# The last group of a dynamic convolution and MLP kernel: its tokens loaded in a turned order by eight DMAs, the last chunk stored by one DMA each

## The chip, the core and the metric

The kernel runs on one core of a Trainium2 chip. TensorE (PE) multiplies matrices, VectorE (DVE) and ScalarE (ACT) do elementwise work, GpSimd (POOL) does little here, and SyncE (SP) issues nearly all DMAs, one after the other, in program order. Sixteen DMA engines move the data. The metric is the device time of one execution in microseconds (us).

## The reference

```python
# x (8, 4096, 192), weight_gen (8, 4096, 8, 7), moe_w_in (192, 2048), moe_w_out (2048, 192), float32
w = softmax(weight_gen, axis=-1)                      # 7 taps for each token and head
out[b, s, h, :] = sum_k w[b, s, h, k] * x_pad[b, s + k, h, :]   # causal, 8 heads of 24 channels
t = out.reshape(32768, 192)
h = t @ w_in
return (relu(h) ** 2) @ w_out                         # (32768, 192) float32
```

Every token gets a weighted sum of itself and its six predecessors, channel by channel, and then goes through a two-layer network with a squared ReLU.

## The kernel before

Token number p*256 + r lies on partition p (of 128) in row r (of R = 256), so each partition holds 256 neighbouring tokens. The work goes in 64 chunks (NCH) of four rows (TC), that is 512 tokens (N). Two chunks share a load group (TG = 8 rows): `load_group(gi)` brings the group's tap logits `wt` (line 116) and its x rows with six rows of halo `xt` (line 117). Two groups' buffers exist. Below, "chunk c" is counted from 0 to 63; chunks 62 and 63 form the last group, gi = 31.

For a chunk, VectorE and ScalarE form the softmax and the tap sums (the convolution). VectorE then transposes blocks (line 402, into `xr`), and SP writes `xr` to a DRAM scratch `xd` (four DMAs, line 408) and reads it back channel-major as `xT` (two DMAs, line 413, which wait until the four have landed). ScalarE splits `xT` into a rounded part `xh` (line 316) and VectorE the remainder `xl` (line 319). These are the moving operands of the first matrix product.

The main loop has eight steps (j) of a chunk. In each, TensorE does `mm1` (line 439, 18 matmuls that read `xh` and `xl` of this chunk) and `mm2_turned` (line 512, 20 matmuls) of the step two back; ScalarE does `relu` (456), `square` (460) and `high` (464), VectorE `low` (468). Every engine runs its instructions in the order written. The convolution of chunk c + 2 is spread from step 3 of chunk c to step 3 of chunk c + 1, its transposes and the DRAM round trip follow, and the split lines 316 and 319 stand in step 6 of the chunk before the one that needs them, ahead of that step's `high`. `load_group((c + 3) // 2)` is issued at step 0 of each odd chunk c; the last group is loaded in chunk 59.

`mm1` and `mm2_turned` read their moving operand through `two_streams`, which takes each run of 32 token columns as two streams of 16 in turn. Each such read therefore moves token 16*i + m of a run of 32 to place 2*m + i. Chunks 1 to 62 are read twice that way; `store_turned` brings their result back through 24 small DMAs (line 540) into `o_sb`, and `put_out` with `reads = 2` undoes the order on the way to DRAM by four DMAs, one for each 32 partitions. The last chunk uses `mm2` with the tokens on the output's partitions, so it has one such read: `store(c, t0, t1)` calls `put_out` with `reads = 1`, again four DMAs. In the last chunk the rows go out in three steps: rows 0 and 1, then row 2, then row 3, each as soon as `finish` has summed it (line 561; for the very last row line 780).

In `put_out` the view `"(q a b r) d -> q b a r d"` makes b the outermost loop of each of the four DMAs: 8 turns for `reads = 2`, 16 for `reads = 1`. Line 77 is its `dma_start`.

Of the kernel before, what the change touches and what calls it, by code (L numbers as in the profile page):

```python
# [21 lines left out]
def kernel(  # L22
# [9 lines left out]
    nc = tc.nc  # L32
# [4 lines left out]
    P = 128  # L37
    Q = 32
    HALO = K - 1
    R = B * S // P  # L40
    PPB = S // R
    TC = 4
    NCH = n_chunks or R // TC
    TG = 8
    CPG = TG // TC
# [26 lines left out]

    def put_out(c, t0, t1, o_sb, reads):
        rows = slice(rows_of(c) + t0, rows_of(c) + t1)
        v = out.rearrange("(q a b r) d -> q b a r d", q=P // Q, a=2 ** reads, r=R)
        for q in range(P // Q):
            nc.sync.dma_start(out=v[q, :, :, rows, :], in_=o_sb[q * Q:(q + 1) * Q, t0:t1])
# [15 lines left out]
    def rows_of(c):  # L93
        return (c + CPG if c < CPG else c - CPG if c < 2 * CPG else c) * TC
# [8 lines left out]
    def load_group(gi):  # L103
        t0 = rows_of(gi * CPG)
        xt = xin.tile([P, TG + HALO, D], F32, name="xt")
        wt = xin.tile([P, TG, H, K], F32, name="wt")
        x_tiles[gi], w_tiles[gi] = xt, wt
        wf = wt.rearrange("p t h k -> p t (h k)")
        if gi == 0:
            nc.sync.dma_start(out=wf[:, 0:TC, :], in_=wg_v[:, t0:t0 + TC, :])  # L110
            nc.sync.dma_start(out=xt[:, HALO:HALO + TC, :], in_=x_v[:, t0:t0 + TC, :])
            for h in (HALO // 2, 0):
                nc.sync.dma_start(out=xt[:, h:h + HALO // 2, :], in_=x_v[:, t0 - HALO + h:t0 - HALO // 2 + h, :])
            return
        if t0 > 0:
            nc.sync.dma_start(out=wf, in_=wg_v[:, t0:t0 + TG, :])
            nc.sync.dma_start(out=xt, in_=x_v[:, t0 - HALO:t0 + TG, :])
            return
        nc.gpsimd.memset(xt[:, 0:HALO, :], 0.0)
        nc.sync.dma_start(out=wf, in_=wg_v[:, 0:TG, :])  # L120
        nc.sync.dma_start(out=xt[:, HALO:, :], in_=x_v[:, 0:TG, :])
        for p0 in range(0, P, PPB):
            nc.sync.dma_start(
                out=xt[p0 + 1:p0 + PPB, 0:HALO, :],
                in_=x_v[p0:p0 + PPB - 1, R - HALO:R, :],
            )
# [398 lines left out]
    def store_turned(c, part):  # L525
        X = works[c]
        if part == 0:
            o_sb = op.tile([P, TC, D], F32, name="o_sb", bufs=2)
            Y = stage.tile([P, 2, N], F32, name="raw")
            outs[c] = o_sb, Y  # L530
            nc.vector.transpose(Y[:, 0], X[:, 0])  # L531
        else:
            nc.vector.tensor_tensor(out=X[0:D1, 1], in0=X[0:D1, 1], in1=X[0:D1, 2], op=ALU.add)
            nc.vector.transpose(outs[c][1][0:D1, 1], X[0:D1, 1])  # L534
        o_sb, Y = outs[c]
        y = Y[:, part].rearrange("p (t q i) -> p q t i" if c < N_PE else "p (q t i) -> p q t i", t=TC, i=Q)
        for e in range(P // Q if part == 0 else D1 // Q):
            d0 = part * P + e * Q
            for q in range(P // Q):
                nc.sync.dma_start(  # L540
                    out=o_sb[q * Q:(q + 1) * Q, :, d0:d0 + Q],
                    in_=y[e * Q:(e + 1) * Q, q],
                )
        if part:
            put_out(c, 0, TC, o_sb, 2)

    outs = {}

# [12 lines left out]
                nc.vector.tensor_tensor(out=to[:, h], in0=acc[:, h], in1=tmp[:, t, l], op=ALU.add)  # L561

    def store(c, t0, t1):
        put_out(c, t0, t1, outs[c][0], 1)


    nc.vector.memset(warm, 0.0)
    nc.scalar.activation(warm, warm, AF.Exp)
    load_group(0)
    eps_terms(0)  # L570
    make_identity(nc, ident)
# [29 lines left out]
    for u in range(NU):  # L601
# [45 lines left out]
        for i in range(3 if u == 0 else 4):  # L647
            relu(0, 4 * u + i)
    load_group(1)
    lace(NU + 1, 1, 2, 3)  # L650
    for f in conv1[3:6]:
# [63 lines left out]
    for c in range(1, NCH):  # L715
        tail = c == NCH - 1
        for j in range(NJ):
            if j == 0 and c % 2 and (c + 3) // 2 * CPG < NCH:
                load_group((c + 3) // 2)
            if j == CONV_BEG and 1 < c < NCH - 2:  # L720
                plan_conv(c + 2, *conv_steps(c + 2, 0))
            if c == 1 and j == 0:
                for t in range(TC // 2):
                    finish(0, t)
                store(0, 0, TC)
# [23 lines left out]
            if c > 1 and j == OUT_STEP:  # L749
                store_turned(c - 1, 0)  # L750
            if c > 1 and j == OUT_STEP + 1:
                store_turned(c - 1, 1)
# [4 lines left out]
    c = NCH - 1  # L757
# [7 lines left out]
    for t in range(TC - 1):  # L765
        for fb in range(NF - 4, NF):
            mm2_tile(c, fb, t)
        finish(c, t)
        if t:
            store(c, 0 if t == 1 else t, t + 1)  # L770
# [7 lines left out]
    o_sb, tmp = outs[c]  # L778
    finish(c, t, tmp[:, t, 0:D])
    nc.vector.tensor_tensor(out=o_sb[:, t], in0=rest[:, 0:D], in1=tmp[:, t, 0:D], op=ALU.add)  # L780
    store(c, t, TC)


# [28 lines left out]
```

## Time and profile before

| | us |
|---|---|
| time of three runs, median | 2145.14 (2144.61 to 2146.45) |
| the profiled execution | 2143.92 |
| its span, first to last instruction | 2142.2 |
| PE busy | 2131.4 (99%) |
| DVE busy | 1857.5 (87%) |
| ACT busy | 1797.9 (84%) |
| mean granted TensorE clock | 0.999 of full speed |

The profiled execution takes 1.7 us more than its span and lies 1.2 us below the median of the runs. A row of a timeline gives the start, the duration, engine, line, operation, what it writes from what, and in brackets the engine's idle time before it and what ended that. SPq is SP's sequencer, where a row is the issue of a DMA, not its transfer. A row of windows gives a stretch, its length, the busy time of each engine with its instruction count, the granted clock, the DMA engines' busy share and the rate in GB/s.

### The profile page before, as it was taken

How to read it: one execution, taken by the hardware profiler on the slowest of the kernel's cores; microseconds unless marked ns; L12 is line 12 of the kernel's file. 1: busy time of each engine (PE TensorE's matmuls, PEld its weight loads, DVE VectorE, ACT ScalarE, POOL GpSimd, SP SyncE). 2: the span in 40 equal slices, each digit the busy share in tenths (PEclk: the TensorE clock that was granted, in tenths of full speed). 3: DMA queues.
4: the chain of work that ended last, by engine and by line, in shares of the span. 5: the costliest groups of instructions: out<-in, count | busy, mean ns of one | idle time of the engine just before them, and what ended most of it. 6: DMA issues, size and time to landing. Idle time of an engine off the chain costs nothing.

```text
span 2142.2 us, 50282 instructions
## 1 busy us (share of the span) xinstructions
PE 2131.4 (99%) x19486; PEld 2044.4 (95%) x19486; DVE 1857.5 (87%) x2866; ACT 1797.9 (84%) x3492; POOL 9.9 (0%) x18
## 2 busy tenths in 40 slices
PE   9999999999999999999999999999999999999998
PEld 9889999999999999999999999999999999999998
DVE  9988988888889888888898888888988888889884
ACT  8888888888888888888888888888888888888886
POOL 0000000000000000000000000000000000000000
PEclk9999999999999999999999999999999999999999
DMA  8433334333233332333433333334333233333231
GB/s 230 100 80 102 88 66 104 88 96 92 62 105 93 91 105 62 93 102 84 103 89 66 104 87 97 91 63 104 91 93 104 62 92 94 91 104 87 67 76 39
DMA packets 324303, 195.33 MB, mean 91 GB/s; under 512 B 225128, under 2 KB 282472, under 8 KB 320224
## 3 DMA queue, kind: packets, MB, share of 16 engines
q1 hardware_dynamic: 322768, 188.58, 34.9%
q0 software_dynamic: 1296, 3.54, 0.9%
q8 instruction: 152, 2.49, 0.5%
q14 instruction: 87, 0.71, 0.1%
HBM read 106.39 MB, written 49.55 MB: 73 GB/s over the span
## 4 chain that ended last, share of the span: by engine, by line
PE 96%; DVE 1%; SPq 1%; ACT 1%; DMA 0%; issue 0%; DVEq 0%; ACTq 0%
PE acc L512 49%; PE ph L439 45%; PE acc L476 1%; PE acc L485 1%; SPq L540 1%; DMA xT<-xd 0%; DVE gl L468 0%; ACT gh L464 0%; ACT rg L460 0%; DMA out_dram<-o_sb 0%; ACT rg L456 0%; DVE du L184 0%; DVE du L186 0%; PE acc L439 0%; DVE xl L319 0%
## 5 line engine op out<-in xcount | busy, mean ns | idle before, releaser
L512 PE MATMUL acc<-gh,V 64*128 64x512 f32 x5952 | 1085.2, 377 | 0.0
L512 PE MATMUL acc<-gl,V 64*128 64x512 f32 x3968 | 917.4, 378 | 0.6 <-DVE gl L468 0.5
L439 PE MATMUL ph<-xh,W 64*128 64x512 f32 x6084 | 917.7, 376 | 0.2
L512 PEld LDWEIGHTS acc<-gh,V 64*128 64x128 f32 x5952 | 779.9, 186 | 25.6
L468 DVE TENSOR_TENSOR gl<-rg,gh 128x512 fp32r<-128x512 f32 x1008 | 641.3, 675 | 119.6 <-ACT gh L464 119.6
L439 PEld LDWEIGHTS ph<-xh,W 64*128 64x128 f32 x6084 | 709.8, 186 | 24.8 <-issue 0.7
L456 ACT ACTIVATE rg<-ph 128x512 f32<-128x512 f32 x992 | 537.8, 594 | 218.1 <-PE ph L439 217.4
L460 ACT ACTIVATE rg<-rg 128x512 f32<-128x512 f32 x1008 | 579.8, 631 | 0.2
L512 PEld LDWEIGHTS acc<-gl,V 64*128 64x128 f32 x3968 | 556.3, 186 | 23.6 <-DVE gl L468 3.3
L464 ACT CAST gh<-rg 128x512 fp32r<-128x512 f32 x1008 | 574.2, 624 | 3.2 <-PE acc L485 3.2
L439 PE MATMUL ph<-xl,W 64*128 64x512 f32 x3042 | 459.3, 376 | 0.0
L275 DVE TENSOR_TENSOR pr<-xt,wt 128x768 f32<-128x768 f32 (+1 forms) x441 | 411.1, 945 | 2.3
L439 PEld LDWEIGHTS ph<-xl,W 64*128 64x128 f32 x3042 | 355.3, 186 | 11.6
L288 DVE TENSOR_TENSOR pr<-pr 128x768 f32<-128x768 f32 x366 | 345.8, 945 | 0.1
L319 DVE TENSOR_TENSOR xl<-xT,xh 128x512 fp32r<-128x512 f32 x186 | 117.5, 687 | 123.0 <-ACT xh L316 120.2
L316 ACT CAST xh<-xT 128x512 fp32r<-128x512 f32 x186 | 102.6, 622 | 1.8 <-DMA xT<-xd 1.7
L246 ACT ACTIVATE wt<-wt 128x224 f32<-128x224 f32 x62 | 24.2, 391 | 94.8 <-DVE wt L245 94.8
L522 DVE TENSOR_TENSOR raw<-acc,raw 128x512 f32<-128x512 f32 x124 | 79.0, 675 | 3.8 <-ACT raw L520 3.8
L520 ACT COPY raw<-acc 128x512 f32<-128x512 f32 x124 | 66.5, 596 | 0.0
L402 DVE STREAM_TRANSPOSE xr<-pr 128x768 f32<-128x768 f32 x62 | 60.7, 978 | 2.1
L534 DVE STREAM_TRANSPOSE raw<-raw 64x512 f32<-64x512 f32 x62 | 43.6, 704 | 2.1
L531 DVE STREAM_TRANSPOSE raw<-raw 128x512 f32<-128x512 f32 x62 | 43.7, 704 | 0.0
(93 smaller groups left out, 450.4 us busy)
## 6 DMA issues: line engine op xcount, KB each, us to landing
xT<-xd SPq DMA_DIRECT2D x124, 384.0 KB
xt<-in_x_dram SPq DMA_DIRECT2D x30, 1344.0 KB
out_dram<-o_sb SPq DMA_DIRECT2D x252, 96.0 KB
xd<-xr SPq DMA_DIRECT2D x248, 96.0 KB
o_sb<-raw SPq DMA_DIRECT2D x1488, 16.0 KB
raw<-raw SPq DMA_DIRECT2D x62, 128.0 KB
wt<-in_weight_gen_dram SPq DMA_DIRECT2D x31, 224.0 KB
raw<-in_moe_w_in_dram SPq DMA_DIRECT2D x16, 192.0 KB
```

The costliest lines, as they stand in the source:

```text
L275: tt(out=dst, in0=src, in1=wf[:, t0 * H:t1 * H, k:k + 1].broadcast_to([P, m, G]), op=ALU.mult)
L288: tt(out=prs[k0], in0=prs[k0], in1=prs.pop(k), op=ALU.add)
L316: nc.scalar.copy(parts["h"][:, k, n], src[k][:, n])
L319: tt(out=parts["l"][:, k, n], in0=src[k][:, n], in1=parts["h"][:, k, n].bitcast(F32), op=ALU.subtract)
L439: nc.tensor.matmul(two[i], w, two_streams(xx[rows, k]), start=(n == 0), stop=(n == len(seq) - 1))
L456: nc.scalar.activation(r, ph, AF.Relu)
L460: nc.scalar.activation(r, r, AF.Square)
L464: nc.scalar.copy(gh, rgs[c, fb])
L468: nc.vector.tensor_tensor(out=gl, in0=rgs.pop((c, fb)), in1=ghs[c, fb].bitcast(F32), op=ALU.subtract)
L512: nc.tensor.matmul(accs[c][b + h], w, two_streams(g[rows]), **fl)
L520: nc.scalar.copy(X[:, k], acc[b])
L522: nc.vector.tensor_tensor(out=X[:, k], in0=acc[b + 1], in1=X[:, k], op=ALU.add)
```

## The change

For the last group alone, `load_group` reads DRAM through `"(q b a r) d -> q a b r d"` with a = 2: within each run of 32 partitions, partition 16*a + b gets the tokens of row block 2*b + a. Logits and x are loaded by four DMAs each, one for every 32 partitions, eight in place of two. After one read through `two_streams` the tokens of chunk 63 then stand in plain order, so `store` calls `put_out` with `reads = 0` for it, a single DMA over 128 partitions. Chunk 62 is read twice, so it now needs `reads = 1`. Chunk 0 keeps `reads = 1`.

```diff
     def put_out(c, t0, t1, o_sb, reads):
         rows = slice(rows_of(c) + t0, rows_of(c) + t1)
+        if reads == 0:
+            nc.sync.dma_start(out=out.rearrange("(p r) d -> p r d", r=R)[:, rows, :], in_=o_sb[:, t0:t1])
+            return
         v = out.rearrange("(q a b r) d -> q b a r d", q=P // Q, a=2 ** reads, r=R)
         for q in range(P // Q):
             nc.sync.dma_start(out=v[q, :, :, rows, :], in_=o_sb[q * Q:(q + 1) * Q, t0:t1])
@@ load_group
+        if gi == NCH // CPG - 1:
+            turned = "(q b a r) d -> q a b r d"
+            x_t = x.rearrange("b s d -> (b s) d").rearrange(turned, q=P // Q, a=2, r=R)
+            wg_t = wg.rearrange("b s h k -> (b s) (h k)").rearrange(turned, q=P // Q, a=2, r=R)
+            for src, dst, r0 in ((wg_t, wf, t0), (x_t, xt, t0 - HALO)):
+                for q in range(P // Q):
+                    nc.sync.dma_start(out=dst[q * Q:(q + 1) * Q], in_=src[q, :, :, r0:t0 + TG, :])
+            return
@@ store_turned
-            put_out(c, 0, TC, o_sb, 2)
+            put_out(c, 0, TC, o_sb, 1 if c >= NCH - CPG else 2)
@@ store
-        put_out(c, t0, t1, outs[c][0], 1)
+        put_out(c, t0, t1, outs[c][0], 1 if c == 0 else 0)
```

## Rows read from the trace of the kernel before

**Rows 1.** The page: the chain that ended last, by engine.

```profile
PE 96%; DVE 1%; SPq 1%; ACT 1%; DMA 0%; issue 0%; DVEq 0%; ACTq 0%
```

**Rows 2.** Timeline of SP's DMA issues, last chunk to the end, and the last issue.

```profile
2112.41 16.15 SPq L540 DMA_DIRECT2D o_sb<-raw  x24
2128.66 10.99 SPq L77 DMA_DIRECT2D out_dram<-o_sb  x16
...
2139.06 0.59 SPq L77 DMA_DIRECT2D out_dram<-o_sb  x1
```

**Rows 3.** Timeline of VectorE at the end: the sums of rows 2 and 3.

```profile
2132.72 0.42 DVE L561 TENSOR_TENSOR o_sb<-acc,raw 128x128 f32<-128x128 f32 x2 [0.72 <-ACT raw L558]
...
2133.69 0.36 DVE L780 TENSOR_TENSOR o_sb<-ph,raw 128x192 f32<-128x192 f32 x1
```

**Rows 4.** Windows after TensorE's last matmul: granted clock and DMA share.

```profile
2137.00:2138.00 1.00, 0.00 (x0) 0.00 (x0) 0.00 (x0) 0.00 (x0) 0.00 (x0) 0.74 0.20 49
2138.00:2139.00 1.00, 0.00 (x0) 0.00 (x0) 0.00 (x0) 0.00 (x0) 0.00 (x0) 0.50 0.10 25
```

**Rows 5.** Timeline of SP's issues in chunk 59, around the last group's load.

```profile
1975.19 0.44 SPq L116 DMA_DIRECT2D wt<-in_weight_gen_dram  x1
1975.67 0.42 SPq L117 DMA_DIRECT2D xt<-in_x_dram  x1
...
1979.14 1.94 SPq L408 DMA_DIRECT2D xd<-xr  x4
1984.61 1.32 SPq L413 DMA_DIRECT2D xT<-xd  x2
```

**Rows 6.** The same view for chunk 60, which has no load.

```profile
2012.09 1.80 SPq L408 DMA_DIRECT2D xd<-xr  x4
2015.61 1.31 SPq L413 DMA_DIRECT2D xT<-xd  x2
```

**Rows 7.** The page's DMA issues: sizes of the transfers.

```profile
xt<-in_x_dram SPq DMA_DIRECT2D x30, 1344.0 KB
...
xd<-xr SPq DMA_DIRECT2D x248, 96.0 KB
...
wt<-in_weight_gen_dram SPq DMA_DIRECT2D x31, 224.0 KB
```

**Rows 8.** Windows in chunk 59 while the load runs: DMA share and GB/s.

```profile
1978.00:1979.00 1.00, 1.00 (x13) 1.00 (x11) 0.97 (x2) 1.00 (x3) 0.00 (x0) 1.00 0.90 366
1979.00:1980.00 1.00, 1.00 (x13) 1.00 (x11) 1.00 (x3) 0.44 (x1) 0.00 (x0) 1.00 1.06 419
...
1983.00:1984.00 1.00, 1.00 (x13) 1.00 (x11) 0.93 (x4) 1.00 (x3) 0.00 (x0) 1.00 0.07 19
```

**Rows 9.** Windows in the output stores: chunk 61's (two rows), chunk 0's (one row).

```profile
2102.50:2102.60 0.10, 0.10 (x4) 0.10 (x2) 0.10 (x1) 0.10 (x2) 0.00 (x0) 1.00 0.60 246
2103.30:2103.40 0.10, 0.10 (x5) 0.10 (x3) 0.10 (x1) 0.10 (x2) 0.00 (x0) 1.00 0.60 246
58.70:58.80 0.10, 0.10 (x4) 0.10 (x2) 0.10 (x1) 0.10 (x1) 0.10 (x1) 1.00 1.44 307
```

**Rows 10.** Timeline of SP and ACT where the split waited for `xT`.

```profile
1391.82 1.32 SPq L413 DMA_DIRECT2D xT<-xd  x2
...
1397.83 1.66 ACT L316 CAST xh<-xT 128x512 fp32r<-128x512 f32 x3 [0.24 <-DMA xT<-xd]
```

**Rows 11.** Timelines of ACT, PE and DVE, end of chunk 59 and start of 60.

```profile
1991.63 1.65 ACT L316 CAST xh<-xT 128x512 fp32r<-128x512 f32 x3
...
1995.68 0.94 PE L439 MATMUL ph<-xh,W 64*128 64x512 f32 x6
...
1997.87 0.48 PE L512 MATMUL acc<-gl,V 64*128 64x512 f32 x2
...
1992.28 1.90 DVE L319 TENSOR_TENSOR xl<-xT,xh 128x512 fp32r<-128x512 f32 x3 [2.01 <-ACT xh L316]
1997.17 1.24 DVE L468 TENSOR_TENSOR gl<-rg,gh 128x512 fp32r<-128x512 f32 x2
```

## What the change was predicted to do, and why

> **What bounds the kernel now.** I read the chain that ended last first: it lies on TensorE for 96% of the span [rows 1], so time can be won or lost in two ways only, by letting TensorE stand idle or by what comes after its last matmul. The second is seen in the timeline of SP's issues at the end, beside that of VectorE. The last sum of the kernel, line 780, ends at 2133.69 + 0.36 = 2134.05 [rows 3], but SP issues its last store only at 2139.06, as the last of 16 issues of line 77 that follow each other without a gap from 2128.66 on, 10.99 / 16 = 0.69 us each [rows 2]. The span ends at 2142.2, so 3.14 us after the last issue. The tail is thus bound by SP's issue rate, for about five us, and the change cuts that count.
>
> The first way needs the chunk in which the load is issued. I looked there for what follows the load in SP's queue: the DRAM round trip of the next chunk's operand, lines 408 and 413 [rows 5], then for the first instruction that needs it (line 316 on ScalarE) and for the first matmul behind that (line 439) [rows 11]. That path has almost no slack, as the next part shows.
>
> **The stores: removed issues.** Chunk 62 keeps four stores, now 16 turns of the outer loop instead of 8. Chunk 63 goes from twelve issues to three. SP comes to chunk 62's stores at 2128.66 and leaves them at about 2128.66 + 4 * 0.69 = 2131.4 [rows 2]. Rows 0 and 1 are summed at 2132.00 (VectorE stood idle for 0.72 before 2132.72) and are issued then; row 2 is summed at 2133.14, row 3 at 2134.05 [rows 3]. Each single issue is over before the next sum, so the last one starts at about 2134.1 in place of 2139.06: 4.96 earlier. It carries four times the data, 98 kB in place of 25: at the 392 GB/s that the load's two steady windows average [rows 8] that is 0.25 against 0.06 us, so 0.2 is given back. **Gain at the end: 4.7 us** (4.2 if a 128-partition issue or its landing takes 0.5 longer than the rows here; 5.0 at most, since the sum of row 3 doesn't move).
>
> **The loads: added issues.** Six more issues at the pitch of 0.48 us (1975.19 to 1975.67) are 2.9 us more of SP [rows 5]. Line 523 was issued behind the load and moves by that much. Line 408 was held by its own input until 1979.14; now SP reaches it at about 1975.67 + 0.47 + 2.9 + 0.6 = 1979.6, half a us later. From line 413's issue to the split, where the split did wait for it, it took 1397.83 - 1391.82 = 6.0 us [rows 10]. So in chunk 59 `xT` was there at 1984.61 + 6.0 = 1990.6 and the split came at 1991.63 [rows 5, 11]: 1.0 us of slack covers the half us. The issues alone cost nothing; without that cover they would cost 0.5.
>
> **The loads: how wide they run.** This is the term that decides. The trace of before holds no load whose outermost loop has two turns, so I bound it from both sides. The store views say how the outermost loop bears on width: while chunk 61's stores run (outer loop 8), the DMA share stands at 0.60 and 246 GB/s in window after window; while chunk 0's run (outer loop 16, the same 3072 bytes for a partition), it goes to 1.44 and 307 GB/s [rows 9]. So the outer loop of 8 kept about half of the engines busy. The turned load walks `a` (2 turns) outermost on its DRAM side. The nearest rows therefore speak for two engines of 16, for each of the eight DMAs, and I take that; the other end is all 16, as for lines 116 and 117, with no cost.
>
> On two engines: the load is 1344 + 224 KB = 1606 kB [rows 7]. The steady windows moved 366 and 419 GB/s, 392 in the mean, 24.5 for one of 16 engines [rows 8]. Two engines move 49 GB/s, so the load lasts 32.7 us (30.6 by the faster window, 35.1 by the slower) in place of some 4. With data flowing about 1.0 us after the first issue, an estimate, it ends at 1975.19 + 1.0 + 32.7 = 2008.9.
>
> The Trainium skill, "DMA: Bandwidth & Descriptors", section "Why a DMA increments its semaphore by 16 and not by 1", says that a DMA issued from SP runs on the largest number of engines up to 16 that divides the outermost counts of both its sides, on the lowest-numbered ones: here two, the same two for all eight DMAs. By that rule the sum is the one above; the trace agrees as far as its stores go (half of the busy share at eight turns), and no run here shows which engines they are.
>
> **What that holds up.** `xr` to `xd` (line 408) goes on the same queue, spread over all engines, so part of each of its four DMAs stands behind the load on those two. In before the load already held it: line 413 came 5.47 us after line 408 with the load ahead and 3.52 without [rows 5, 6]. Now, after 2008.9, the two engines still have their sixteenth each of lines 523 and 408 to move, 1.3 us at 24.5 GB/s (four DMAs of 96 KB [rows 7] and, by the code, 64 partitions of 512 floats), and line 413 followed the last traffic of 1983 to 1984 by under a us [rows 5, 8]; I take 0.8. Line 413 is issued at 2011.0 in place of 1984.61, and `xT` is there 6.0 later, at 2017.0. The split at 1991.63 becomes 2017.0: **25.4 us late**.
>
> On ScalarE everything of chunk 59's last two steps is queued behind that split, on VectorE line 319 and all behind it. TensorE can go on to 1995.68, where chunk 60's first `mm1` wants `xh` [rows 11]. It then stands idle until 2017.6. Of the 25.4, nothing is absorbed: in before the first `gl` that `mm2` needs after that `mm1` was ready at 1997.17 + 0.7 = 1997.87, and its matmul started at 1997.87 [rows 11]. VectorE's chain from the split to it is unchanged, so that matmul moves by the full 25.4.
>
> The clock: after TensorE's last matmul the granted clock went from 1.00 (2.4 GHz) to 0.50 (1.2 GHz) within the window 2137 to 2138, less than 4.5 us after the engine stopped [rows 3, 4]. A pause of 21.9 us will do the same. At half rate chunk 60's first `mm1` takes 3.9 us instead of 1.94 and still ends before the `gl` that comes next, at 2023.3; so that much is covered. How much longer the clock stays low no row shows: between nothing and one step at half rate, 4.1 us (a chunk of eight steps is 2012.09 - 1979.14 = 32.95 [rows 5, 6]). I take nothing.
>
> A second stall isn't due: after line 413 SP has chunk 58's 24 small DMAs, four stores and line 523 to catch up on, 16.15 + 2.8 + 0.6 us [rows 2], and is free at 2032, before the next line 408 at 2012.09 + 25.4. x of the last group is wanted from step 3 of chunk 60 on, later than it lands.
>
> **Sum.** +25.4 - 4.7 = +20.7 us. Against the profiled execution (2143.92, span 2142.2 and 1.7 around it) 2164.6; that execution lies 1.2 below the median of the runs, so 2165.8, and I predict 2166.
>
> **Rivals.** First, *the load is spread over all engines* after all, because what counts is the SBUF side with its 32 partitions. Then the added issues are hidden as shown, and only the tail remains: 2145.14 - 4.7 = 2140.4, 0.22% faster. For it: transfers of 32 partitions stand all over the trace (lines 408, 540). Against it: chunk 61's stores have 32 partitions on the SBUF side too, and ran at half width [rows 9]. It decides where the load ends by 1991.63 - 6.0 - 2.1 = 1983.5 with the steps of the sum, so from nine engines up. The Trainium skill, same page, "Rules for kernel authors", says of two transfers to disjoint halves of the partitions that both still spread over all 16 engines; by that rule it would be this case, and the stores' rows speak against it.
>
> Second, *the two engines change from DMA to DMA*, or the queue lets line 408 past the load. With four pairs at work the load lasts 1606 kB / 196 GB/s = 8.2 us, line 413 comes at 1975.19 + 1.0 + 8.2 + 2.1 = 1986.5, the split at 1992.5 in place of 1991.63: 0.9 late. That gives 2145.14 - 4.7 + 0.9 = 2141.3, within 0.2%. For it only that no row tells the engines apart; against it that line 408 did wait behind the load in before [rows 5, 6].
>
> **How the numbers follow.** About 0.2% (4.3 us) is what a measurement of this kernel can tell from no change. The forecast gets 0.85, the first rival 0.08, half of it beyond 0.2% faster and half within; the second 0.06, 0.05 of that within 0.2% and 0.01 faster; another stall that I don't see 0.01. So faster 0.05, same 0.09, slower 0.86. The range is that of the forecast: low with the faster window's rate, data 0.4 us sooner and the full 5.0 of the tail, 2145.14 + 25.4 - 2.5 - 5.0 = 2163, less a few us for a shorter way from `xd` to the split, 2159; high with the slower rate, the clock's 4.1 and a tail of 4.2, 2145.14 + 25.4 + 2.4 + 4.1 - 4.2 = 2173, with 1 for the spread of the runs 2174.
>
> **What would show it.** In the changed profile: the DMA share in chunk 59 stands near 2/16 for some 30 us; line 413's issue comes near 2011; line 316 is preceded by a long idle time ended by the DMA `xT<-xd`; TensorE has one gap of over 20 us at chunk 60's first `mm1`, with the granted clock at 0.50 in it; and at the end the last line 77 is issued within 0.2 us of line 780's end. If the share reaches 1 during the load, the first rival holds and the time is near 2140. If the gap is there but the tail still shows issues without a gap, the stores' term is wrong.

## The result and the profile after

The changed kernel takes 2165.49 us, the median of four runs (2163.88 to 2167.15), against 2144.88 (2144.23 to 2146.45) for the kernel before. The ratio is 1.0095, with a 95% interval from 1.0078 to 1.0113: slower by 20.6 us. Lines have moved: 408, 413 and 316 of before are 419, 424 and 327 of after; 439 is 450, 512 is 523, 468 is 479, 540 is 551; the new load is line 124, a store of four DMAs is line 80 and the single store line 76.

The profiled execution of after took 2167.15, with a span of 2165.4. It was already 3.6 us behind the profiled execution of before where it came to the load (first issue at 1978.80, in before at 1975.19 [rows 5]), in a stretch where the two programs are the same. Times below are therefore compared from the first issue of the load on.

The page of after, the chain that ended last by engine, answers to [rows 1]. TensorE's share has gone from 96 to 89%, and DMA and VectorE have taken it.

```profile
PE 89%; DVE 4%; DMA 3%; ACT 2%; SPq 1%; issue 1%; DVEq 0%; ACTq 0%
```

The timeline of SP's issues in chunks 59 and 60 of after answers to [rows 5, 6]: start, duration, line, what is written from what, and the number of issues.

```profile
1978.80 2.65 SPq L124 DMA_DIRECT2D wt<-in_weight_gen_dram  x4
1981.49 2.53 SPq L124 DMA_DIRECT2D xt<-in_x_dram  x4
1984.12 0.58 SPq L534 DMA_DIRECT2D raw<-raw  x1
1985.13 14.90 SPq L419 DMA_DIRECT2D xd<-xr  x4
2013.44 1.31 SPq L424 DMA_DIRECT2D xT<-xd  x2
2014.85 16.56 SPq L551 DMA_DIRECT2D o_sb<-raw  x24
2031.51 3.09 SPq L80 DMA_DIRECT2D out_dram<-o_sb  x4
2034.65 0.56 SPq L534 DMA_DIRECT2D raw<-raw  x1
2040.55 1.80 SPq L419 DMA_DIRECT2D xd<-xr  x4
```

The eight issues take 5.2 us, and that isn't the loss. The four issues of line 419 right behind them take 14.90 us, where the next chunk's take 1.80, and line 424 is issued 34.6 us after the first issue of the load; in before it was 9.4 [rows 5].

The chain that ended last of after, from there on, says what the time went on: the landing of line 419's DMAs, not their issue, is the long piece.

```profile
1994.04 19.33 DMA xd<-xr
...
2013.44 0.66 SPq L424
...
2014.16 5.85 DMA xT<-xd
...
2020.09 0.63 ACT xh L327
```

Windows of after over the same stretch (columns: stretch, length, busy time of PE, PEld, DVE, ACT and POOL, granted clock, DMA share, GB/s) show how wide the load ran.

```profile
1980.00:1985.00 5.00, 5.00 (x49) 5.00 (x48) 4.39 (x8) 2.63 (x6) 0.00 (x0) 1.00 0.12 41
...
2005.00:2010.00 5.00, 0.00 (x0) 0.00 (x0) 0.00 (x0) 0.00 (x0) 0.00 (x0) 0.50 0.13 54
...
2024.00:2025.00 1.00, 1.00 (x8) 0.68 (x6) 0.97 (x2) 1.00 (x3) 0.00 (x0) 0.50 0.13 20
2025.00:2026.00 1.00, 0.52 (x4) 0.00 (x0) 1.00 (x2) 1.00 (x3) 0.00 (x0) 0.84 0.19 30
2026.00:2027.00 1.00, 0.67 (x6) 0.62 (x8) 1.00 (x3) 1.00 (x3) 0.00 (x0) 1.00 0.18 28
```

A DMA share of 0.12 to 0.13 is two engines of sixteen, where the load of before stood at 0.90 to 1.06 [rows 8]. That they are the same two throughout is seen in the packets of line 419's four DMAs. The DMA view of after counts those of the windows 1994 to 1996 and 2010 to 2013.5:

```profile
DMA packets 192, 0.19 MB, mean 97 GB/s; under 512 B 14, under 2 KB 182, under 8 KB 182
DMA packets 122, 0.13 MB, mean 37 GB/s; under 512 B 12, under 2 KB 108, under 8 KB 116
```

A DMA of 96 KB goes as 192 packets of 512 bytes. In the first window one of the four moves 182 - 14 = 168 of them, fourteen sixteenths, beside ten packets of the load (over 8 KB); the small ones under 512 B carry no data to speak of. The missing two sixteenths of all four DMAs, 96 packets, move only in the second window (108 - 12), where the load ends. So fourteen engines were free at once and the same two were held to the end. All compute engines have stopped by the window from 2005. The timelines of TensorE and ScalarE of after show the gap; they answer to [rows 11].

```profile
1998.91 0.51 PE L523 MATMUL acc<-gl,V 64*128 64x512 f32 x2
2020.76 1.84 PE L450 MATMUL ph<-xh,W 64*128 64x512 f32 x6 [21.34 <-ACT xh L327]
...
2026.33 0.48 PE L523 MATMUL acc<-gl,V 64*128 64x512 f32 x2 [0.81 <-DVE gl L479]
```

```profile
2020.09 1.66 ACT L327 CAST xh<-xT 128x512 fp32r<-128x512 f32 x3 [24.90 <-DMA xT<-xd]
```

TensorE runs dry, waits 21.34 us for `xh`, and ScalarE, which would make `xh`, has waited 24.90 us for the DMA `xT<-xd`. It is one stall in one place: on the page of after all but 0.2 us of the 21.5 us that TensorE idled ahead of line 450 is this gap.

The end of after, in the timelines of SP and of VectorE, answers to [rows 2, 3].

```profile
2157.27 2.56 SPq L80 DMA_DIRECT2D out_dram<-o_sb  x4
2160.78 2.37 SPq L76 DMA_DIRECT2D out_dram<-o_sb  x3
...
2162.82 0.33 SPq L76 DMA_DIRECT2D out_dram<-o_sb  x1
```

```profile
2162.43 0.36 DVE L791 TENSOR_TENSOR o_sb<-ph,raw 128x192 f32<-128x192 f32 x1
```

The last sum ends at 2162.79 and the last store is issued at 2162.82. From that sum to the end of the span it is 2.6 us; in before it was 2142.2 - 2134.05 = 8.15 [rows 3].

### The profile page after: what moved, and what is told of

It reads as the page before. It is cut to its first block, busy times and chain, and to the rows that moved or that the text cites. A ratio compares the mean times of both kernels' runs of the same rounds, so it can differ in the third digit from the quotient of the medians.

```text
span 2165.4 us, 50281 instructions
## 1 busy us (share of the span) xinstructions
PE 2134.2 (99%) x19486; PEld 2044.1 (94%) x19486; DVE 1857.2 (86%) x2866; ACT 1797.6 (83%) x3492; POOL 9.9 (0%) x18
## 4 chain that ended last, share of the span: by engine, by line
PE 89%; DVE 4%; DMA 3%; ACT 2%; SPq 1%; issue 1%; DVEq 0%; ACTq 0%
PE acc L523 45%; PE ph L450 41%; DMA xT<-xd 1%; PE acc L487 1%; DVE gl L479 1%; DMA xd<-xr 1%; DVE pr L299 1%; PE acc L496 1%; DVE xl L330 1%; DVE pr L286 1%; SPq L551 1%; ACT rg L467 1%; ACT gh L475 0%; ACT rg L471 0%; SPq L419 0%
## 5 line engine op out<-in xcount | busy, mean ns | idle before, releaser
L450 PE MATMUL ph<-xh,W 64*128 64x512 f32 x6084 | 919.1, 377 | 21.5 <-ACT xh L327 21.3
```

Of the source, the lines that this page charges most:

```text
L450: nc.tensor.matmul(two[i], w, two_streams(xx[rows, k]), start=(n == 0), stop=(n == len(seq) - 1))
```

## The experiments

All ratios are to the kernel before, timed on the same chip beside the experiment, where it took 2147.02 us (for e1 to e4) or 2146.70 (for e5 to e9). The theory: the stall comes from the load's narrow spread, which two turns of its outermost loop bring about, and the stores gain what SP no longer has to issue. The rivals on trial are that the number of DMAs, the scattered order in DRAM, or the place of the issue is to blame.

**The two parts, each alone.** `e1_stores_only` drops the branch in `load_group`, so that the last group comes by lines 116 and 117 as before; `e2_load_only` takes the old stores back.

```diff
# e1_stores_only, against after
-        if gi == NCH // CPG - 1:
...
-            return
# e2_load_only, against after
-            put_out(c, 0, TC, o_sb, 1 if c >= NCH - CPG else 2)
+            put_out(c, 0, TC, o_sb, 2)
-        put_out(c, t0, t1, outs[c][0], 1 if c == 0 else 0)
+        put_out(c, t0, t1, outs[c][0], 1)
```

> The changed stores without the turned load: the last group is loaded by two plain DMAs as before, so the rows of the last two chunks leave in another order than the reference's; the amount of work is the same. Theory (the loss is all in the load, the gain all in the stores): no gap on TensorE in chunk 59, and only the shorter tail is left. The changed kernel ends 2165.4 - 2162.79 = 2.6 us after its last sum, before 2142.2 - 2134.05 = 8.15, so 5.5 us less: 2144.9 - 5.5 = 2139.4 us. Rival (the single-DMA stores are themselves slow, or the tail is given back elsewhere): 2144 us or more.

> The turned load alone, with the stores as before, so the rows of the last two chunks leave in another order than the reference's; the amount of work is the same. Theory: the whole stall and none of the tail's gain, 2144.9 + 25.4 to 26 = 2170 to 2171 us, with one gap of over 20 us on TensorE before chunk 60's first product. Rival (part of the loss belongs to the stores): no more than 2166 us.

The stores alone: 2141.57 us, ratio 0.9974 (0.9965 to 0.9983), 5.5 us faster. The load alone: 2170.77, ratio 1.0111 (1.0095 to 1.0127), 23.8 slower. SP's issues at the end of the stores alone, then its last sum on VectorE:

```profile
2131.27 2.56 SPq L80 DMA_DIRECT2D out_dram<-o_sb  x4
2134.99 2.37 SPq L76 DMA_DIRECT2D out_dram<-o_sb  x3
...
2137.03 0.33 SPq L76 DMA_DIRECT2D out_dram<-o_sb  x1
```

```profile
2136.65 0.36 DVE L783 TENSOR_TENSOR o_sb<-ph,raw 128x192 f32<-128x192 f32 x1
```

The span ends at 2140.0, 3.0 us after that sum. The load alone, TensorE's and SP's timelines:

```profile
2020.59 1.84 PE L450 MATMUL ph<-xh,W 64*128 64x512 f32 x6 [21.14 <-ACT xh L327]
```

```profile
2157.24 10.70 SPq L80 DMA_DIRECT2D out_dram<-o_sb  x16
```

The gap of 21.14 us stands in the load alone and not in the stores alone; the sixteen issues in one run at the end stand in the load alone. So both signs of the sum are shown. Their sum, 18.3 us, lies 2.3 below the 20.6 of the whole, which is within the intervals; an effect of one part on the other smaller than that isn't ruled out. The expected times started from 2144.9 for the kernel before, which took 2147.02 here, so the differences are what to compare: -5.5 expected and -5.5 measured for the stores, +25 to +26 expected and +23.8 (20.4 to 27.3) measured for the load.

**How many turns.** `e5_outer_4` leaves eight loads of the same size and changes only the turned view, four turns outermost for two.

```diff
-            x_t = ... rearrange(turned, q=P // Q, a=2, r=R)
-            wg_t = ... rearrange(turned, q=P // Q, a=2, r=R)
+            x_t = ... rearrange(turned, q=P // Q, a=4, r=R)
+            wg_t = ... rearrange(turned, q=P // Q, a=4, r=R)
```

> The turned view of the load with a = 4 instead of 2, so that the outermost loop has four turns; the bytes and the eight DMAs are the same, the last two chunks' tokens are mixed differently, so the output's last rows differ. Theory (an outermost loop of c turns keeps the DMA on c engines and the scratch DMAs wait behind it): the load takes 1606 kB / (4 x 24.5 GB/s) = 16.4 us instead of 32.7, TensorE's gap shrinks by as much, from 21 to about 5 us, and the time is before + 25 - 16 - 5.5 = before + 3 to 4 us. Rival (the turned addresses or the eight issues are slow, the loop count doesn't matter): before + 20 us, as the changed kernel.

It took 2151.33 us, ratio 1.0023 (1.0013 to 1.0033), 4.6 slower. Its SP timeline, TensorE's gap and a window while the load runs:

```profile
1979.61 2.67 SPq L124 DMA_DIRECT2D wt<-in_weight_gen_dram  x4
...
1986.05 3.83 SPq L419 DMA_DIRECT2D xd<-xr  x4
2000.69 1.31 SPq L424 DMA_DIRECT2D xT<-xd  x2
```

```profile
2007.94 1.83 PE L450 MATMUL ph<-xh,W 64*128 64x512 f32 x6 [7.65 <-ACT xh L327]
```

```profile
1995.00:2000.00 5.00, 5.00 (x49) 4.89 (x46) 0.00 (x0) 1.05 (x3) 0.00 (x0) 1.00 0.24 94
```

With the same eight issues the DMA share goes from 0.13 to 0.24, and line 424 comes 21.1 us after the load's first issue where it came 34.6 after. The share is turns over sixteen in both, and the gap follows it. The expected gap of about 5 us and loss of 3 to 4 were both too small, by 2.7 and about 1 us. Neither the number of DMAs nor their bytes have changed, so the turns are the cause of the stall. The order in DRAM, which changes with them, isn't: in the window from 2005 of after, where nothing but the load moved, its two engines moved 54 GB/s, 27 each, no less than the 24.5 of one engine in before [rows 8]. (The rate in GB/s of a window counts other DMAs too.) The Trainium skill, "DMA: Bandwidth & Descriptors", section "Why a DMA increments its semaphore by 16 and not by 1", has the number of engines as the largest up to 16 that divides the slowest counts of both sides; the shares at two and at four turns agree. The Trainium skill, same section, also has the lowest-numbered engines for a DMA from SP, the same each time; the packets of line 419 above agree that they were the same two, and no run shows which they are.

**Sixteen turns, by sixteen loads.** If width were all, sixteen turns would hide the load. `e3_sixteen_loads` cuts each load in two of 16 partitions, so that the loop over b, with 16 turns, is outermost; `e7_plain_sixteen` does the same cut in plain order of DRAM.

```diff
# e3_sixteen_loads
-                    nc.sync.dma_start(out=dst[q * Q:(q + 1) * Q], in_=src[q, :, :, r0:t0 + TG, :])
+                    for h in range(2):
+                        p0 = q * Q + h * (Q // 2)
+                        nc.sync.dma_start(out=dst[p0:p0 + Q // 2], in_=src[q, h, :, r0:t0 + TG, :])
# e7_plain_sixteen
+            for src, dst, r0 in ((wg_v, wf, t0), (x_v, xt, t0 - HALO)):
+                for p0 in range(0, P, Q // 2):
+                    nc.sync.dma_start(out=dst[p0:p0 + Q // 2], in_=src[p0:p0 + Q // 2, r0:t0 + TG, :])
```

> The same turned order, but each of the eight loads is cut into its two turns of a: sixteen DMAs of 16 partitions, whose outermost loop has 16 turns on both sides. Theory (the load is slow because an outermost loop of two keeps it on two engines): the load runs on all engines and takes about 4 us, the DMA share goes to about 1 during it; SP has 14 issues more than before, 14 x 0.48 = 6.7 us, so line 408's four go out some 4.3 us later, less 1.0 of slack, so up to 3.3 us are lost and 5.5 won: 2139.4 to 2142.7 us. Rival (the turned addresses in DRAM are slow in themselves, or the number of issues is what costs): 2160 us or more.

> The sixteen loads of 16 partitions again, but in plain token order, with the changed stores, so the last rows leave in another order than the reference's. It tells why the sixteen turned loads moved only 102 to 150 GB/s at a DMA share near 1. Theory A (sixteen engines that write into 16 neighbouring partitions hinder each other): the same low rate and the same stall of some 4.5 us, before + 1 us. Theory B (the turned addresses, two partitions' rows apart in DRAM, are slow): the plain ones run at 350 GB/s or more, line 426's issue comes 4 us after line 421's and little is left of the stall: before - 4 to before - 1.

The turned sixteen took 2148.37 us, ratio 1.0012 (1.0002 to 1.0021); the plain sixteen 2147.78, ratio 1.0009 (0.9999 to 1.0018). Both still have the quicker end, so, against the 5.5 us that the stores alone gain, both lose 6 to 7 us to the load. Neither expectation of the first was met; the second came out as its theory A. A window of each while the load runs, the turned one first, and TensorE's gap in each:

```profile
1985.00:1990.00 5.00, 5.00 (x50) 5.00 (x48) 4.08 (x8) 4.99 (x10) 0.00 (x0) 1.00 0.97 127
```

```profile
1985.00:1990.00 5.00, 5.00 (x50) 5.00 (x48) 3.32 (x7) 4.99 (x11) 0.00 (x0) 1.00 1.04 140
```

```profile
2001.90 1.84 PE L452 MATMUL ph<-xh,W 64*128 64x512 f32 x6 [4.54 <-ACT xh L329]
```

```profile
2003.45 1.84 PE L447 MATMUL ph<-xh,W 64*128 64x512 f32 x6 [3.69 <-ACT xh L324]
```

The gaps are less than the loss: the first products behind them took twice as long too (1.84 for 0.94 [rows 11]), and ScalarE's split came 24.0 and 23.7 us after the load's first issue, 7.6 and 7.3 later than in before [rows 5, 11].

The share of all sixteen engines is near 1 now, at 127 to 140 GB/s; in before they moved 366 to 419 at the same share [rows 8]. The order in DRAM isn't the reason, since plain order does the same. What the two loads share, and before has not, is that each DMA goes to 16 neighbouring partitions, and that there are sixteen of them. In the turned sixteen the windows from 1984 to 1991 have 84 packets of over 8 KB at a share of 0.98, so each held an engine for 0.98 * 16 * 7 / 84 = 1.3 us; from 1978 to 1980 in before it was 0.98 * 16 * 2 / 73 = 0.43. The packets themselves are slow, which speaks for the partitions and against the count of DMAs; no run parts the two. The Trainium skill, "SBUF — State Buffer", section "Door 1: The DMA port swizzle", says that a transfer's rate goes with how many of SBUF's 16 ports its partitions reach, and gives 104 GB/s for 16 neighbours, which reach four; the runs agree in kind, but their 127 to 140, nearly all of it the load's, lies above that figure, and none of them moved the same bytes to 16 spread partitions to show it alone.

**Another queue.** `e4_gpsimd_loads` issues the eight turned loads from GpSimd.

```diff
-                    nc.sync.dma_start(out=dst[q * Q:(q + 1) * Q], in_=src[q, :, :, r0:t0 + TG, :])
+                    nc.gpsimd.dma_start(out=dst[q * Q:(q + 1) * Q], in_=src[q, :, :, r0:t0 + TG, :])
```

> The eight turned loads unchanged in shape, but issued by GpSimd, whose queue holds nothing else at this time, instead of SP. Theory (the stall comes from the scratch DMAs standing behind the load in SP's queue): lines 419 and 424 are no longer held and the stall is gone or a few us at most, 2139.4 to 2143 us, even if the load itself still takes long. Rival (the two engines are what is full, whatever queue the DMAs come from): line 419's share on these engines still waits, and the time is 2155 us or more.

It took 2150.36 us, ratio 1.0015 (1.0006 to 1.0024), 3.3 slower. GpSimd isn't held by SP's order and issued the load a chunk earlier, as soon as the buffers came free. Its timelines on GpSimd, SP and TensorE, and a window while the load runs:

```profile
1945.29 2.45 POOL L124 DMA_DIRECT2D wt<-in_weight_gen_dram  x4 [1858.90 <-DVE pr L286]
1947.86 2.33 POOL L124 DMA_DIRECT2D xt<-in_x_dram  x4
```

```profile
1948.97 2.87 SPq L419 DMA_DIRECT2D xd<-xr  x4
...
1963.28 1.32 SPq L424 DMA_DIRECT2D xT<-xd  x2
```

```profile
1970.51 1.84 PE L450 MATMUL ph<-xh,W 64*128 64x512 f32 x6 [4.70 <-ACT xh L327]
```

```profile
1953.00:1954.00 1.00, 1.00 (x13) 1.00 (x11) 0.93 (x4) 1.00 (x3) 0.00 (x0) 1.00 0.65 187
```

Neither expectation was met, and the run moved the load in time as well as to another queue. The same eight DMAs with two turns ran far wider here: in the windows from 1949 to 1962 the share, other DMAs included, is 0.27 to 0.99, and line 424 came 18.0 us after the load's first issue where it came 34.6. So two engines for a DMA doesn't mean the same two for all of them when GpSimd issues. Yet the scratch write of chunk 58, issued in the middle of the load, had its read follow only 14.3 us later (3.5 where no load runs [rows 6]): a queue of its own doesn't keep one transfer out of the other's way. Whether they met at the engines or at SBUF stays open.

**Another place.** `e9_load_later` issues after's turned load behind line 424 of chunk 59, in that chunk's step 3.

```diff
-            if j == 0 and c % 2 and (c + 3) // 2 * CPG < NCH:
+            g = (c + 3) // 2
+            if c % 2 and g * CPG < NCH and j == (CONV_BEG if g == NCH // CPG - 1 else 0):
```

> The changed kernel with the eight turned loads moved behind the scratch round trip of chunk 59 in SP's order (issued at step 3, after line 424). The load still lasts some 32 us on two engines. Theory (the stall is whatever stands behind the load in SP's queue): chunk 60's split is no longer held, but SP's next 24 small DMAs now stand behind the load. If SP may issue on while they wait, the next round trip (line 419 at about 2012) waits only for the load's end near 2020 and 3 to 5 us are lost: about before. If SP itself is stopped by full queues, as the issue times of line 419 in the changed kernel hint (14.9 us for four), the next round trip is issued some 20 us late and TensorE stands idle in chunk 60 instead: before + 13 to + 17. Rival (the loss has nothing to do with what is behind the load): before + 20, with the gap still at chunk 60's first product.

It took 2163.62 us, ratio 1.0075 (1.0059 to 1.0092), 16.9 slower. SP's issues and TensorE's gap:

```profile
1984.68 2.72 SPq L124 DMA_DIRECT2D wt<-in_weight_gen_dram  x4
1987.45 2.55 SPq L124 DMA_DIRECT2D xt<-in_x_dram  x4
1990.14 40.89 SPq L551 DMA_DIRECT2D o_sb<-raw  x24
...
2034.89 2.06 SPq L419 DMA_DIRECT2D xd<-xr  x4
2038.75 1.32 SPq L424 DMA_DIRECT2D xT<-xd  x2
```

```profile
2045.56 1.83 PE L450 MATMUL ph<-xh,W 64*128 64x512 f32 x6 [17.40 <-ACT xh L327]
```

The stall isn't hidden, it moves one chunk on; this is the second case of the theory, at the upper end of its 13 to 17 us. Chunk 60's operand is now in time, but SP can't get past line 551: its 24 issues take 40.89 us, where they take 16.15 in before [rows 2]. Only seven of them were out before 2019.69; the load's last packets (over 8 KB) are in the window from 2018 to 2019, and the other seventeen issues followed in 11.35 us. So SP was held until the load had drained, and came to chunk 60's line 419 as late as that.

**The gain without the load.** `e8_undo_in_split` loads in plain order and turns the last chunk's tokens in the split instead, where ScalarE and VectorE read them in another order at the same number of elements; chunk 62 keeps its old stores. The diff shows the split alone; chunk 63's stores are those of after.

```diff
+        def halves(t):
+            return t.rearrange("p (b i m) -> p b i m", i=2, m=Q // 2) if c == NCH - 1 else t
+        def turned(t):
+            return t.rearrange("p (b m i) -> p b i m", i=2, m=Q // 2) if c == NCH - 1 else t
-            nc.scalar.copy(parts["h"][:, k, n], src[k][:, n])
+            nc.scalar.copy(halves(parts["h"][:, k, n]), turned(src[k][:, n]))
-            tt(out=parts["l"][:, k, n], in0=src[k][:, n], in1=parts["h"][:, k, n].bitcast(F32), op=ALU.subtract)
+            h = halves(parts["h"][:, k, n].bitcast(F32))
+            tt(out=halves(parts["l"][:, k, n]), in0=turned(src[k][:, n]), in1=h, op=ALU.subtract)
```

> No turned load: the last group is loaded by two plain DMAs as before, and chunk 63's order is undone where ScalarE and VectorE split its operand (they read the transposed columns in the turned order, three free dimensions in place of one, the same count of elements). The stores are those of the changed kernel for chunk 63; chunk 62 keeps its four stores with reads = 2. Theory (all of the loss is in the load, all of the gain in the stores of chunk 63): no gap on TensorE, the tail 5.5 us shorter, before - 5 to - 5.5. Rival (the turned reads of the split are slow and hold ScalarE in chunk 62's step 6): up to 2 us of it given back.

It took 2142.25 us, ratio 0.9973 (0.9964 to 0.9982): 4.5 us faster than the kernel before. ScalarE's timeline has its price, and SP's its end:

```profile
2095.33 1.81 ACT L325 CAST xh<-xT 128x512 fp32r<-128x512 f32 x3
```

```profile
2136.90 2.38 SPq L76 DMA_DIRECT2D out_dram<-o_sb  x3
```

The three casts take 1.81 us in place of the 1.65 of the plain ones [rows 11], and VectorE's three subtractions the 1.90 that they took before [rows 11]; TensorE waits 0.4 us at most from the load on. The 4.5 is half a us short of the 5 to 5.5 expected, and its interval, 3.9 to 7.7, holds both. This is about what the change had to give once the order is undone where no DMA has to walk it.

## Why the prediction was right

The predicted 2166.0 stands beside 2165.49 measured, and the sign came from the term that was said to decide.

**Width.** Taken from stores of eight and sixteen turns [rows 9], two turns were read as two engines, the same two each time. The share of 0.12 to 0.13 and the packets of line 419 show it, and the four-turn run shows that the turns set it. The prediction's 0.60 and 1.44 came from single windows of 0.1 us (the two beside that of 1.44 have 0.75 and 0.51); over 2102.25 to 2102.75 the eight-turn stores of before stand at 0.49, eight engines of sixteen, which bears its reading out better than the rows it used. The first rival (all engines) had to bring the share to 1, the second (changing pairs) to about half; neither came on SP's queue. On GpSimd's the share looks like the second one's mechanism, though no run shows which engines they were.

**From the load to the split.** First issue to line 424: predicted 2011.0 - 1975.19 = 35.8 us, measured 34.6. Line 424 to the split: 6.0 predicted, 6.65 measured. Together 41.8 predicted and 41.3 measured. In before the split came 16.4 us after the first issue [rows 5, 11], so it is 24.9 us late where 25.4 was predicted. Two errors of about a us cancelled there by half: the two engines were somewhat quicker than the mean of the windows, and the read back somewhat slower than the one row I took.

One part of that path had another form than I said. I let SP issue line 408 in 1.94 us and two sixteenths of its DMAs wait behind the load. Those did wait, but SP itself was also stopped for most of 14.90 us in issuing them. The time to line 424 is the same, since the same two engines had to drain, but with other work behind it that would have been a second loss, as the later load shows.

**TensorE's gap and the clock.** A gap of 21.9 us was predicted, from the first product to the split; measured are 21.34, and 0.81 more ahead of `gl`. The granted clock fell to 0.50 in the gap and stayed there until the window 2025 to 2026, some five us after the restart, which no row of before could tell. I took its cost as nothing because the wait for `gl` would cover it, and it did: the first product's group took 1.84 us instead of 0.94 [rows 11], TensorE still waited 0.81 for `gl`, and the matmul on `gl` stands 2026.33 - 1978.80 = 47.53 us behind the load's first issue where it stood 1997.87 - 1975.19 = 22.68 [rows 5, 11]. That is 24.85 late, exactly as late as the split.

**No second stall.** SP was predicted free at 2032, ahead of the next line 419 at 2012.09 + 25.4 = 2037.5. It was free at 2034.65 + 0.56 = 2035.2 and that line came at 2040.55, each 3.1 to 3.2 us later, less than the 3.6 that the execution had lost before. The four issues took 1.80 us, so nothing held them.

**The tail.** This is the term that was mis-sized. Predicted were 4.7 us, "5.0 at most"; the profiles of before and after give 8.15 - 2.6 = 5.5, the stores alone gave 5.5 by the medians and 8.15 - 3.0 = 5.2 by their profile. The cap rested on the sum of row 3 not moving, which is so, and on holding the 3.14 us from the last issue to the end as they were, plus 0.2 for the bytes. They became 2165.4 - 2162.82 = 2.58 in after and 2140.0 - 2137.03 = 2.97 in the stores alone. The issue itself is 0.26 shorter (0.33 in place of 0.59 [rows 2]), which is all of the 0.17 won there by the stores alone and about half of the 0.56 in after. The charge for the four times larger data isn't seen. Whether the store over 128 partitions also lands sooner is not shown: in the load alone, where the last store still covers 32, the end came 2.75 us after its issue, 0.4 less than in before with the same stores.

**The sum.** 25.1 us at the last sum (28.74 later, less the 3.6 that the execution had already lost) less 5.5 is 19.6 in these two executions, and 20.6 by the medians, against 20.7 predicted. The us between them is in the spread of the runs, which is 3.3 for after, so that the forecast came within half a us of the median is luck; that the two terms are right to about a us each is not.

## What to carry over

A reordered view of a DMA costs more than its descriptors: the count of its outermost loop set how many DMA engines it used on SP's queue (two turns two, four turns four), and the wide transfers behind it landed only after the narrow one. Before an order is turned in a load, see whether an elementwise pass that is there anyway can read it turned: here that cost 0.16 us of ScalarE and kept the gain to within the noise. At the end of a kernel, count the issues behind the last sum, not the bytes.

## What the runs showed of the hardware

- Behind the eight loads on two engines four DMAs of 96 KB moved fourteen sixteenths of their packets at once, and the last two sixteenths (96 packets) only when the load had ended.
- The issue of a DMA can itself stand still. Behind the load on two engines four issues took 14.90 us (1.80 without), and with the load moved 24 issues took 40.89 (16.15). So in both runs a slow transfer held back what SP had to issue next, other tiles' work included.
- Sixteen engines at a share of 0.97 to 1.04 moved 127 to 140 GB/s where each DMA went to 16 neighbouring partitions, in turned and in plain order, and in the turned run a packet of x held its engine 1.3 us in place of 0.43; the share alone doesn't tell that a load runs well.
- Eight DMAs with two turns ran at a share of 0.12 to 0.13 from SP, and of 0.27 to 0.99 from GpSimd.
- After the pause of 21 us TensorE's granted clock was still 0.50 (1.2 GHz) in the window from 2024 to 2025, after over three us of matmuls, and 1.00 (2.4 GHz) in the one from 2026.
